# LayerNorm statistics of one token tile moved to ScalarE, and two of three warm-up matmuls taken out of a transformer block's prologue

## The chip, the cores and the metric

One core of a Trainium2 chip. The metric is the device time of one execution in microseconds (us). A time quoted here is a median of several executions; the profile is that of one execution, and its span is 1.7 to 1.9 us shorter than that execution's time (805.0 us of span went with 806.83 us). "Granted clock" is the mean share of TensorE's full speed over an execution. The experiments were made in five calls on four chips, each call with the kernel before beside them, so times are compared within a call. Every execution counts as fast; for e7 and e8, one execution each, the state is unknown.

## The reference

One block: attention with 32 heads of 16 columns over 2048 tokens of 512 columns, then a gated MLP, both behind a LayerNorm that is scaled and shifted by six vectors made from a condition `c`.

```python
def reference(A_x, A_wqkv, A_wo, B_x, B_w_gate, B_w_up, B_w_down, c, w_mod):
    x = A_x
    mod = (_silu(c) @ w_mod).reshape(c.shape[0], 6, 1, -1)
    sa, ca, ga, sb, cb, gb = ...                      # six vectors of 512
    h = _layernorm(x, axis=-1) * (1 + ca) + sa
    x = x + ga * attention(h, A_wqkv, A_wo)           # H = 32, Dh = 16, softmax over 2048 keys
    h = _layernorm(x, axis=-1) * (1 + cb) + sb
    x = x + gb * (_gelu(h @ w_gate) * (h @ w_up) @ w_down)
    return x
```

## The kernel before

The program is written as one stream of recorded operations. A small model of the engines orders them on the host ahead of time. In the main loop ScalarE takes the exponentials of all scores (686 instructions, most of 1024 or 1536 columns), while TensorE makes scores and value products. The prologue has to produce the first scores: LayerNorm of four token tiles of 128 rows, the modulation columns, transposes, the first projections.

```python
        self.warm_up(7)
        # ... cut: identity and masks on GpSimd
        for dc in range(NDC):
            self.mm(self.scp[:, 0, dc:dc + 1], self.crow[0:1, P * dc:P * dc + P], self.ones[0:1, 0:1])
        self.warm_up(14)
        self.act(self.tcol[:, :], self.scp[:, 0, 0:NDC], ACT.Tanh, scale=0.5)
        for t in range(2):
            self.ln_stat(t)                     # VectorE: statistics of tiles 0 and 1
        self.ln_rstd(0, 2)                      # GpSimd: 1 / standard deviation
        # ... cut: silu of c
        for t in range(2, 4):
            self.ln_stat(t)                     # VectorE: tiles 2 and 3
        self.ln_rstd(2, 4)
        self.mod_cols(self.scp[:, 1, 0:8], 0)   # TensorE: 32 products, wait for w_mod
        for t in range(4):
            self.ln_norm(t, self.tb1[:, 0, t, :])
        self.copy(dve, self.modA[:, :], self.scp[:, 1, 0:8])
        self.ts(dve, self.modA[:, 4:8], self.modA[:, 4:8], 1.0, None, ALU.add)
        self.warm_up(3)
        # ... cut: 16 transposes, each group of 4 followed by its modulation; then the projections

    def warm_up(self, n):
        for _ in range(n):
            self.mm(self.mi[:, :], self.warm[:, 0:P], self.warm)   # becomes 4 quarter products of 512 columns

    def ln_stat(self, t, src=None):
        s6 = self.st6[:, t % 2, :]
        self.bn_stats(s6, self.xs[:, t, :] if src is None else src)
        self.bn_aggr(self.mv[:, t, :], s6)
```

One part of the host's model of TensorE matters later. It counts every matmul (`fetched[0]`, from 0) and lets every 128th start no sooner than 3750 ns after the 128th before it:

```python
            if self.fetched[0] % 128 == 0 and t > 20000:
                t = self.fetched[1] = max(t, self.fetched[1] + 3750)
            self.fetched[0] += 1
```

So a change of the number of matmuls in the prologue changes what this model expects, and with it the order that it chooses, some 750 us later.

## Time and profile before

| | before |
|---|---|
| time, median of 3 (lowest to highest) | 807.34 us (806.82 to 807.36) |
| span of the profiled run | 805.0 us |
| first exponential starts | 13.51 us |
| ScalarE busy, TensorE busy | 96%, 93% of the span |
| modulation columns start (TensorE), "M" below | 7.66 us |

The profile is read as follows. The chain that ended last says what the end waited for. A timeline row is start, length, engine, source line, operation, the tile written and the tile read, shapes, count, and in brackets how long the engine stood idle ahead of it and what released it; `<-issue` means that no semaphore wait explains the idle time. Names of tiles: `xs` tokens, `st` and `mv` statistics, `dreg` the normalized tokens (and the warm-ups' operand), `sc_bf,mreg` the modulation columns, `hreg,wreg` the first projections, `ps_pv<-E,vaug` value products, `ps_sc<-xs,ident` fillers of the main loop. A warm-up group of 4 quarter products takes 0.43 us while the array runs at half clock and 0.22 us at full clock. The lines themselves stand in the prediction.

### The profile page before, as it was taken

To read this page: it belongs to the slowest core of one execution; us is meant where nothing else is said; L and a number is where in the kernel's file an instruction comes from. 1 tells how busy PE (TensorE), PEld (TensorE's weight loads), DVE (VectorE), ACT (ScalarE), POOL (GpSimd) and SP (SyncE) were. 2 spreads that over 40 slices of the span, in tenths; PEclk is the share of its full clock that TensorE was granted. 3 is DMA by queue.
4 is the path that set the end of the run, shared out by engine and by line. 5 is a ranking of instruction groups with operands and counts; after the bars stand their busy time and mean duration, and the time that the engine had idled before them with its cause. 6 is when DMAs were issued, how large, how long until landed. Compare 5 with 4: busy or idle time off the path is not lost.

```text
span 805.0 us, 27412 instructions
## 1 busy us (share of the span) xinstructions
PE 749.6 (93%) x12250; PEld 267.6 (33%) x12254; DVE 671.0 (83%) x1216; ACT 773.7 (96%) x728; POOL 277.7 (34%) x172
## 2 busy tenths in 40 slices
PE   8899999998899999999999899999999899999987
PEld 3333333322222222222222222222344342454455
DVE  7878898978898989988688998989778986677873
ACT  5999999999999999999999999999999999999982
POOL 3110335365546172456556346134262010000310
PEclk9999999999999999999999999999999999999999
DMA  9101000000022121111003111110123221120100
GB/s 310 58 9 19 10 10 16 10 16 10 16 55 68 35 55 36 48 41 29 24 27 108 36 52 51 48 42 17 42 59 89 63 75 37 34 75 14 23 9 14
DMA packets 58632, 36.03 MB, mean 45 GB/s; under 512 B 17977, under 2 KB 55090, under 8 KB 58514
## 3 DMA queue, kind: packets, MB, share of 16 engines
q1 hardware_dynamic: 56914, 32.84, 15.0%
q8 instruction: 96, 1.57, 0.8%
q10 hardware_dynamic: 1600, 1.44, 0.6%
q14 instruction: 22, 0.18, 0.1%
HBM read 29.62 MB, written 2.61 MB: 40 GB/s over the span
## 4 chain that ended last, share of the span: by engine, by line
ACT 89%; PE 8%; DVE 3%; issue 0%; DVEq 0%
ACT E L381 85%; PE ps_sc L368 4%; ACT wreg L381 3%; PE ps_mi L368 3%; PE ps_pv L368 1%; DVE mreg L393 1%; DVE kmo L402 0%; DVE xs L385 0%; DVE wreg L385 0%; PE ps_sc L372 0%; DVE hreg L393 0%; ACT L381 0%; DVE vaug L402 0%; DVE dreg L393 0%; DVE kme L393 0%
## 5 line engine op out<-in xcount | busy, mean ns | idle before, releaser
L381 ACT ACTIVATE E<-ps_sc 128x1024 bf16<-128x1024 f32 (+2 forms) x686 | 748.2, 1282 | 15.6 <-PE ps_sc L368 15.0
L393 POOL TENSOR_SCALAR mreg<-dreg 128x2048 uint16<-128x2048 uint16 x93 | 175.3, 1902 | 260.7 <-DVE mreg L393 105.7
L393 DVE TENSOR_SCALAR dreg<-ps_sc 128x512 uint16<-128x512 f32 x253 | 171.6, 685 | 34.3 <-PE ps_sc L368 31.8
L368 PE MATMUL ps_sc<-qT,kme 32*128 32x512 bf16 (+2 forms) x1313 | 168.3, 332 | 18.3 <-ACT E L381 15.1
L368 PE MATMUL ps_sc<-qT,kmo 32*128 32x512 bf16 (+2 forms) x1313 | 173.7, 332 | 9.7 <-ACT E L381 8.5
L368 PE MATMUL ps_pv<-E,vaug 128*17 128x512 bf16 (+2 forms) x2112 | 150.4, 327 | 0.8 <-DVE osb L402 0.5
L393 POOL TENSOR_SCALAR mreg<-mreg 128x2048 uint16<-128x2048 uint16 x46 | 86.7, 1902 | 138.8 <-DVE mreg L393 47.1
L368 PE MATMUL ps_pv<-mreg,vaug 128*17 128x512 bf16 (+2 forms) x1704 | 121.6, 337 | 1.7 <-DVE mreg L393 1.0
L393 DVE TENSOR_SCALAR mreg<-ps_sc 128x512 uint16<-128x512 f32 x126 | 85.4, 686 | 18.9 <-PE ps_sc L368 17.5
L368 PE MATMUL ps_mi<-wreg,mreg 128*32 128x512 bf16 (+1 forms) x1280 | 92.4, 372 | 4.4 <-DVE wreg L398 1.3
L368 PEld LDWEIGHTS ps_sc<-qT,kme 32*128 32x128 bf16 x1313 | 45.0, 91 | 143.7 <-ACT E L381 115.4
L368 PEld LDWEIGHTS ps_sc<-qT,kmo 32*128 32x128 bf16 x1313 | 45.7, 91 | 127.8 <-ACT E L381 109.3
L393 DVE TENSOR_SCALAR mreg<-dreg 128x2048 uint16<-128x2048 uint16 x117 | 76.8, 682 | 1.7 <-PE ps_pv L368 1.4
L368 PEld LDWEIGHTS ps_pv<-E,vaug 128*17 128x17 bf16 x2112 | 43.9, 89 | 61.5 <-issue 48.8
L368 PEld LDWEIGHTS ps_pv<-mreg,vaug 128*17 128x17 bf16 x1704 | 38.1, 89 | 36.8 <-issue 13.2
L402 DVE CAST wreg<-ps_mi 128x512 bf16<-128x512 f32 x49 | 33.5, 684 | 10.5 <-PE ps_mi L368 10.3
L368 PEld LDWEIGHTS ps_mi<-wreg,mreg 128*32 128x32 bf16 x1280 | 26.7, 95 | 44.0 <-issue 18.8
L368 PE MATMUL ps_mi<-hreg,wreg 128*32 128x512 bf16 x480 | 39.5, 385 | 0.0
L393 DVE TENSOR_SCALAR mreg<-mreg 128x2048 uint16<-128x2048 uint16 x59 | 38.4, 682 | 1.1 <-PE ps_pv L368 1.0
L398 DVE SCALAR_TENSOR_TENSOR wreg<-wreg,ps_mi 128x512 bf16<-128x512 bf16 x49 | 33.4, 682 | 6.5 <-PE ps_mi L368 5.1
L635 POOL TENSOR_SCALAR mv<-mv 128x4 f32<-128x4 f32 (+2 forms) x11 | 2.6, 239 | 94.5 <-DVE mv L425 93.9
L385 DVE TENSOR_TENSOR wreg<-wreg 128x1024 bf16<-128x1024 bf16 (+1 forms) x56 | 34.1, 616 | 0.5
(149 smaller groups left out, 670.8 us busy)
## 6 DMA issues: line engine op xcount, KB each, us to landing
mreg<-in_B_w_up_dram SPq DMA_DIRECT2D x22, 256.0 KB, 2.9
mreg<-in_B_w_gate_dram SPq DMA_DIRECT2D x15, 256.0 KB, 3.0
rb<-scr_rec SPq DMA_DIRECT2D x96, 32.0 KB, 1.8
dreg<-in_B_w_down_dram SPq DMA_DIRECT2D x9, 256.0 KB, 3.0
mreg<-in_w_mod_dram SPq DMA_DIRECT2D x1, 2048.0 KB, 13.3
mreg<-in_B_w_down_dram SPq DMA_DIRECT2D x8, 256.0 KB, 2.7
out_dram<-xs SPq DMA_DIRECT2D x16, 128.0 KB, 1.7
osb<-osb SPq DMA_DIRECT2D x48, 32.0 KB, 2.0
```

Of the source, the lines that this page charges most:

```text
L368: return self.rec("pe", lambda e: e.matmul(out, lhsT, rhs, start=start, stop=stop, tile_position=tp), [lhsT, rhs], [out], cost=(n, int(rhs ...
L381: return self.rec("act", lambda e: e.activation(out, in_, func, scale=scale, **kw), rd, wr, cost=self.cost("act", out, [in_], "act"))
L385: return self.rec(eng, lambda e: e.tensor_tensor(out, a, b, op), [a, b], [out], cost=self.cost(eng, out, [a, b], "tt"))
L393: return self.rec(eng, lambda e: e.tensor_scalar(out, a, s1, s2, **kw), rd, [out], cost=self.cost(eng, out, [a], "ts"))
L398: return self.rec("dve", lambda e: e.scalar_tensor_tensor(out, a, s, b, op0=op0, op1=op1), rd, [out], cost=self.cost("dve", out, [a, b], " ...
L402: return self.rec(eng, lambda e: e.tensor_copy(out, in_), [in_], [out], cost=self.cost(eng, out, [in_], "ts"))
L635: self.rec("pool", lambda e: e.tensor_scalar(v, v, EPS, None, op0=ALU.add), [v], [v], cost=200)
```

## The change

The intent: the statistics of tile 3 are the last on VectorE; ScalarE is idle then and can make a sum and a sum of squares with its accumulating output, so that VectorE has three tiny instructions left. The warm-ups ahead of the transposes then would be the only thing in the way, so two of three go. Both parts aim at an earlier first exponential.

```diff
         self.act(self.tcol[:, :], self.scp[:, 0, 0:NDC], ACT.Tanh, scale=0.5)
+        self.act(self.E[:, 0, :], self.xs[:, 3, :], ACT.Copy, accum=self.rden[:, 0, 0:1])
+        self.act(self.E[:, 0, :], self.xs[:, 3, :], ACT.Square, accum=self.rden[:, 0, 1:2])
 ...
-        for t in range(2, 4):
-            self.ln_stat(t)
+        self.ln_stat(2)
+        m, q, v = self.rden[:, 0, 0:1], self.rden[:, 0, 1:2], self.mv[:, 3, 1:2]
+        self.ts(dve, self.mv[:, 3, 0:1], m, 1.0 / D, None, ALU.mult)
+        self.stt(v, m, 1.0 / D, self.mv[:, 3, 0:1], ALU.mult, ALU.mult)
+        self.stt(v, q, 1.0 / D, v, ALU.mult, ALU.subtract)
         self.ln_rstd(2, 4)
 ...
-        self.warm_up(3)
+        self.warm_up(1)
```

The order of instructions also changes near the end (767 us), because the host's model counts 8 matmuls fewer.

In the prediction, the marked cuts are statements that no trace or run of this case shows. No term of its sum rests on them: it stays 0.37 + 0.24 = 0.61 us, 806.73 us in all, and the 0.70 us taken for each of ScalarE's two instructions is from the trace (695 ns).

> **What bounds the kernel now.** I read the page first (busy shares, then the chain that ended last), then that chain in order of time for the first 32 us and for the last 50, then the timelines of VectorE, GpSimd, TensorE and ScalarE in those two stretches.
>
> The page, busy line of ScalarE and the chain by engine:
>
> ```profile
> span 805.0 us, 27412 instructions
> ...
> ACT 89%; PE 8%; DVE 3%; issue 0%; DVEq 0%
> ```
>
> ScalarE's exponentials set the time: 89% of the chain. They can't start before the prologue has produced the first scores, so the prologue's length (first exponential at 13.51 us) is added to the whole, and whatever shortens it should come off the end one for one. Between 13 and 70 us the view of waits lists no wait for a DMA, so no arrival is there to swallow an earlier start. The chain in the prologue:
>
> ```profile
> 4.59 3.13 PE ps_mi L368 x56
> 7.73 0.89 PE ps_sc L368 x32
> 8.62 0.76 PE ps_mi L368 x12
> 9.38 1.00 PE ps_sc L372 x16
> 10.38 0.39 PE ps_pv L368 x4
> ```
>
> TensorE alone is named: 14 warm-ups, the 32 columns of the modulation, three more warm-ups (12 quarter matmuls), 16 transposes, projections. But the timeline of VectorE and GpSimd shows a second path that ends almost together with it:
>
> ```profile
> 6.43 0.18 DVE L425 BATCH_NORM_AGGREGATE mv<-st 128x2 f32<-128x6 f32 x1
> 6.53 0.66 DVE L421 BATCH_NORM_STATS2 st<-xs 128x6 f32<-128x512 bf16 x1
> 7.22 0.18 DVE L425 BATCH_NORM_AGGREGATE mv<-st 128x2 f32<-128x6 f32 x1
> 7.49 0.30 POOL L635 TENSOR_SCALAR mv<-mv 128x2 f32<-128x2 f32 x1 [0.85 <-DVE mv L425]
> 7.88 0.73 POOL L637 TENSOR_TENSOR rstd<-mv,half 128x2 f32<-128x2 f32 x1
> 8.64 0.74 DVE L393 TENSOR_SCALAR dreg<-xs,mv,rstd 128x512 bf16<-128x512 bf16 x2 [0.61 <-POOL rstd L637]
> 9.29 0.16 DVE L402 COPY modA<-ps_sc 128x8 f32<-128x8 f32 x1
> 9.48 0.17 DVE L393 TENSOR_SCALAR modA<-modA 128x4 f32<-128x4 f32 x1
> 9.76 1.00 DVE L393 TENSOR_SCALAR hreg<-ps_sc,modA 128x512 bf16<-128x512 bf16 x2
> ```
>
> Statistics of tile 3 end at 7.40, rstd of tiles 2 and 3 at 8.61, their norms at 9.05 and 9.38, modA at 9.65. And TensorE in two narrow windows, around 9.0 and 9.48:
>
> ```profile
> 8.99 0.39 PE L368 MATMUL ps_mi<-dreg 128*32 128x512 bf16 x4
> ...
> 9.31 0.40 PE L372 MATMUL ps_sc<-ident,dreg 128*128 128x128 bf16 x4
> ```
>
> The third warm-up starts at 8.99 and takes 0.2 us of issue; the transposes start at 9.31, some 0.06 apart, the fourth at 9.49, when tile 3's norm (9.38) had been ready for 0.1 us. So the warm-ups set the transposes, with the statistics path 0.05 us behind; the fourth's end (9.71) releases the modulate at 9.76. Neither part of the change can give much alone.
>
> One more place, near the end: the chain there, and one filler of the main loop.
>
> ```profile
> 754.72 12.23 ACT E L381 x11
> 766.94 0.04 issue
> 766.98 0.78 PE ps_sc L368 x11
> ...
> 767.99 9.99 ACT E L381 x8
> ```
> ```profile
> 766.98 0.62 PE L368 MATMUL ps_sc<-xs,ident 128*32 128x512 bf16 x8 [0.52 <-ACT E L381]
> 767.53 0.23 PE L368 MATMUL ps_sc<-qT,kme 32*128 32x128 bf16 x3
> ```
>
> Two filler products (8 quarter matmuls) stand between the release of a score buffer and the scores that ScalarE needs next. Exponentials of 1024 columns follow each other at 0.90 us (765.78, 766.68); the next could have started at 767.59, and started at 767.98.
>
> [...] The trace has 598 ns from PSUM and 695 ns for a 128x512 tile in SBUF; I take 0.70. [...] Built, the changed kernel has the same two table loads as before, so none is added (1.28 us each in this trace). [...] in the trace a dependent small instruction starts 0.19 us after the one before (9.29 to 9.48). [...] the trace agrees on the two speeds (first 7 warm-ups 3.1 us, 0.43 each; the next 14 take 3.13, 0.22 each).
>
> **The change part by part.** (a) Off VectorE: tile 3's statistics, 0.66 + 0.18 us, at 6.53 to 7.40.
>
> (b) On ScalarE: Copy and Square of tile 3 with sums. ScalarE is idle from 4.80 to 9.97. The tile's DMA was issued at 1.21 and landed 3.5 us later, at 4.71. So the Copy runs 4.80 to 5.50, the Square, which waits for it, about 5.55 to 6.25; with an unknown cost for each sum, by 6.6. VectorE needs the first sum at 6.53 and the second at 6.91: hidden.
>
> (c) On VectorE instead: three dependent 128x1 instructions, at 6.53, 6.72, 6.91, ending near 7.07. GpSimd gets its input at 7.07 instead of 7.40: -0.33 us. Then as before: 0.09 + 0.30 + 0.09 + 0.73, rstd at 8.28; norms at 8.31 and 8.64, ending 8.72 and 9.05; modA copy at 8.96, plus one at 9.15, ending 9.32.
>
> (d) TensorE: one warm-up at 8.54 (0.22) plus the 0.11 seen before the transposes gives the first at 8.87; the fourth waits for tile 3's norm: 9.05 + 0.06 = 9.11, ending 9.33. The modulate starts at 9.38, when modA is ready too. That is 9.76 - 9.38 = 0.38 us earlier. The warm-ups cut alone would leave the fourth transpose at 9.38 + 0.06 = 9.44 (-0.05); the statistics alone would leave it at 9.49 (0).
>
> (e) After it nothing new: the K weights landed at 2.17 + 7.3 = 9.47, before the first projection's new time of 9.98. First exponential at about 13.14. I count 0.37 us.
>
> (f) The order of instructions, from the built kernels: identical on every engine after the prologue up to about 767 us. There the static scheduler leaves out the two fillers at 766.98, and VectorE does one score conversion ahead of a small product and another small product earlier. Without the fillers the scores start at 766.98; their third bank waits for a conversion that ends at 767.00, so they are complete near 767.45 and ScalarE can start at 767.59: up to 0.39 us. But TensorE then is busy without a gap to the scores at 770.15, and the filler there (768.09) still waits for the exponential that ends at 767.85. It moves only to 767.90, so those scores come 0.19 us earlier, complete near 770.42, and the exponential that was at 770.66 starts there: 0.24 us of the 0.39 stay. From 767.98 to 777.98 ScalarE has no gap, and the tail follows it.
>
> Sum: 0.37 + 0.24 = 0.61. 807.34 - 0.61 = 806.73 us.
>
> **The rivals.** First, the prologue's gain is lost because the warm-ups were needed: with fewer columns between 7.7 and 10.0 us the clock could halve for one window, in which the projections (1.76 us) would take twice as long. For it: little else runs on the array there. Against it: the stretch that starts at 11 us is no busier and kept 0.22 us per group. The time would be 807.5 to 809, perhaps in some runs only. Second, ScalarE's sums come late (a hidden cost of reading them out, or a later landing of tile 3), and VectorE waits: each 0.1 us past 6.9 costs 0.1; at 0.3 late the prologue gives nothing, and the time is 807.1. Third, the gap at 767 closes less because a VectorE conversion comes later in the new order: prologue alone, 806.97. Fourth, all 0.39 stays: 806.58.
>
> **Range and chances.** The three runs before spread over 0.54 us, near the size of the gain, so the median carries some 0.2 of noise. With the rivals, 806.2 to 807.3 should hold it 8 times in 10; most of the rest lies above. Two per cent is 16 us; no mechanism here reaches it. I give faster 0.005, within 2% 0.985, slower 0.01 for something unforeseen.
>
> **What would show it.** In the profile after: Square ending before 6.9; the last small statistics instruction ending near 7.07; rstd at 8.3; modulate at 9.4; first exponential near 13.1; the exponential at 767.98 now near 767.2 (both shifts together) and the last one 0.6 earlier. Projections at 0.43 us per group would prove the clock rival. A wait of VectorE for ScalarE ahead of the small instructions would prove the second. A first exponential at 13.1 with an unchanged end would mean that a fixed arrival took the gain back, and the statement on DMA waits would be wrong.

## The result, and the profile after

| | before, same call | after |
|---|---|---|
| time, median of 4 | 807.35 us (806.82 to 807.46) | 807.39 us (806.53 to 808.79) |
| ratio of fast runs, 95% interval | | 1.0003, 0.9986 to 1.0021 |
| span of the profiled run | 805.0 us | 806.9 us |
| M, first exponential, distance | 7.66, 13.51, 5.84 us | 8.21, 13.62, 5.41 us |
| from the first exponential to the end | 791.45 us | 793.33 us |

A ratio here is the mean time of one kernel's fast runs over that of the other's in the same rounds, so it isn't quite the ratio of the medians beside it. The change isn't seen in the time at all; 806.73 us was predicted, and the measured median lies 0.09 us above the upper end of the range of 806.2 to 807.3.

The page of the kernel after (the span, the queue of kind "instruction", the shares of the chain that ended last):

```profile
span 806.9 us, 27386 instructions
...
q8 instruction: 96, 1.57, 0.8%
...
ACT 86%; PE 9%; DVE 3%; DMA 1%; SPq 1%; issue 0%; DVEq 0%
```

ScalarE still carries the chain, but DMA and the sequencer of SyncE are new in it with 1% each. The chain in order of time, kernel after, prologue (start, length, what):

```profile
4.61 3.67 PE ps_mi L368 x56
8.27 0.88 PE ps_sc L368 x32
9.16 0.33 PE ps_mi L368 x4
9.49 1.00 PE ps_sc L372 x16
10.49 0.37 PE ps_pv L368 x4
```

The third row has 0.33 us where the kernel before had 0.76: the two warm-ups are gone, and what follows M is shorter by 0.43 us. But the first row is longer by 0.54 us (3.67 after 3.13). Same work, 14 groups, but ten of the first 21 groups ran wholly or partly at half clock in this execution and seven in the other (the granted clock doubled at 5.66 us here and at 4.29 us there). That lies ahead of the changed part, and in this one execution it took the gain back before that part had begun.

ScalarE's timeline in the kernel after, with the two sums:

```profile
4.79 0.63 ACT L381 ACTIVATE E<-xs 128x512 bf16<-128x512 bf16 x1
5.33 0.19 ACT L381 ACTIVATION_READ_ACCUMULATOR E<-xs 128x1 f32 x1
5.54 0.63 ACT L381 ACTIVATE E<-xs 128x512 bf16<-128x512 bf16 x1
6.08 0.19 ACT L381 ACTIVATION_READ_ACCUMULATOR E<-xs 128x1 f32 x1
```

Each sum is read out by an instruction of its own, 0.19 us; all is over at 6.27. And VectorE in the kernel after, the three tiny instructions, the norms and the modulation vector:

```profile
6.32 0.12 DVE L393 TENSOR_SCALAR mv<-rden 128x1 f32<-128x1 f32 x1
6.47 0.35 DVE L398 SCALAR_TENSOR_TENSOR mv<-rden,mv 128x1 f32<-128x1 f32 x2
...
8.09 0.73 DVE L393 TENSOR_SCALAR dreg<-xs,mv,rstd 128x512 bf16<-128x512 bf16 x2 [0.61 <-POOL rstd L642]
9.20 0.17 DVE L402 COPY modA<-ps_sc 128x8 f32<-128x8 f32 x1 [0.38 <-PE ps_sc L368]
```

No wait for ScalarE stands ahead of them, the statistics end at 6.82 and the last norm at 8.82. VectorE then waits 0.38 us for TensorE's modulation columns: in this execution the statistics path isn't near the critical path any more.

To see where the later time went, the k-th exponential of one trace was set beside the k-th of the other (both have 686), and the lag of the kernel after was followed. These are the steps over 0.2 us, and the first and the last lag:

```
exponential   start before   start after   lag
0                13.51         13.62       0.11
221, 222        248.82, 249.73 249.56, 251.08   0.12 -> 1.35
667 to 669      763.45 - 765.78  764.88 - 767.70  1.23 -> 1.92
671             767.98        769.52       1.94 -> 1.55
676             774.65        776.56       1.67 -> 1.91
end             804.96        806.95       1.99
```

At 248 us the array runs a window at half clock (granted clock 0.5 for 3.41 us), in the middle of the unchanged main loop: eight fillers take 1.03 us, 0.61 in the kernel before. At 671 is the predicted gain of two missing fillers, -0.39 us. The step at 676 goes with a round trip of the softmax denominators through memory, one leg of which took 3.3 us in this trace; its cause was not tested (e4 below has a step of 0.28 us there too, behind a stall of 0.60 us at the 11842nd matmul). At 667 to 669 is something else. TensorE's timeline in the kernel after:

```profile
762.13 0.34 PE L368 MATMUL ps_pv<-E,vaug 128*17 128x128 bf16 x10
763.13 0.28 PE L368 MATMUL ps_pv<-E,vaug 128*17 128x128 bf16 x6 [0.66 <-issue]
...
766.29 0.35 PE L368 MATMUL ps_pv<-E,vaug 128*17 128x128 bf16 x12
766.87 0.23 PE L368 MATMUL ps_pv<-E,vaug 128*17 128x128 bf16 x4 [0.23 <-issue]
```

and the first of these two runs of 16 value products in the kernel before:

```profile
760.97 0.60 PE L368 MATMUL ps_pv<-E,vaug 128*17 128x128 bf16 x16
```

After the change the same run of products is broken in two, with 0.66 us of idle time in its middle and no semaphore that it waits for. The stall comes at matmul number 11458 of the trace, counted from 0, the next one at number 11586: 128 apart. In the kernel before, the run took 0.60 us where its neighbours take 0.40: number 11458 lies in it too, near its start, and came 0.20 us after the matmul before it. These stalls are what the experiments had to explain.

### The profile page after: what moved, and what is told of

Same layout as the page of the kernel before. It is cut to its first block, busy times and chain, and to the rows that moved or that the text cites. A ratio compares the mean times of both kernels' runs of the same rounds, so it can differ in the third digit from the quotient of the medians.

```text
span 806.9 us, 27386 instructions
## 1 busy us (share of the span) xinstructions
PE 750.0 (93%) x12234; PEld 267.4 (33%) x12238; DVE 671.3 (83%) x1217; ACT 775.8 (96%) x732; POOL 277.4 (34%) x172
## 3 DMA queue, kind: packets, MB, share of 16 engines
q8 instruction: 96, 1.57, 0.8%
## 4 chain that ended last, share of the span: by engine, by line
ACT 86%; PE 9%; DVE 3%; DMA 1%; SPq 1%; issue 0%; DVEq 0%
ACT E L381 83%; PE ps_sc L368 4%; PE ps_mi L368 3%; ACT wreg L381 3%; PE ps_pv L368 1%; DVE mreg L393 1%; SPq L432 1%; DMA scr_rec<-rden 0%; DMA den<-scr_den 0%; DMA rb<-scr_rec 0%; DVE kmo L402 0%; DVE xs L385 0%; DVE dreg L393 0%; PE ps_mi L372 0%; DVE wreg L385 0%
```

## The experiments

Eighteen runs were made; all were correct. "Stretch" is the time from the first exponential to the end in the profiled run, "M" the start of the modulation columns. Comparing M, M to first exponential, and stretch keeps apart what the times mix. Each of these three comes from one execution of each kernel.

### 1. Are these two traces typical? The same kernels again, and each half of the program alone

e1 is the kernel before without an edit, e2 the kernel after. e3 and e4 use the fact that the host's model only counts matmuls: shifting its count by 8 gives the end order of one kernel to the other.

```diff
# e3: prologue before, end order after        # e4: prologue after, end order before
         self.prologue()                               self.prologue()
+        self.fetched[0] -= 8                 +        self.fetched[0] += 8
         self.stream()                                 self.stream()
```

> The kernel before, unchanged, as a control. All theories: ratio 1.000 to the kernel before, within what the rounds scatter. Its trace gives a second look at when the array's clock doubles in the warm-ups: if the doubling comes at another moment than 4.5 us, the first exponential moves from 13.51 us by 0.21 us per slow group of four warm-up matmuls (theory A, a clock phase that differs from run to run); if it stays at 13.51 whatever the phase, theory A falls.

> The changed kernel, unchanged. Theory A (both steps of the prediction are real and each about as large as predicted; the single profiled run hid them behind a late doubling of the clock, 0.55 us, one slow clock window at 248 us, 1.24 us, and late denominators near the end, 0.8 us): ratio about 0.9993 (-0.6 us), 0.9989 to 0.9997. Theory B (the filler's gain is swallowed by the wait for the denominators' round trip; the prologue's is real): -0.37 us, 0.9995. Theory C (8 matmuls fewer ahead of everything shift where TensorE's stream of instructions stalls, and stalls at 762 and 766 us now lie on the path in every run): ratio about 1.000, with TensorE waits of 0.6 us marked as issue at the same two places.

> The kernel before with only the order near the end as in the changed kernel (two fillers fewer, one conversion and one product moved), prologue untouched. Theory A: -0.24 us, ratio 0.9997, and in the trace the exponential after the missing fillers 0.39 us closer to the one before it, of which the exponential two places on gives back 0.15. Theory B: the same step in the trace, but ScalarE waits that much longer for the scores behind the denominators at about 774 us: ratio 1.000. Theory C: 1.000, no stall at 762.

> Both parts of the change in the prologue, with the order near the end kept as before. Theories A and B: -0.37 us, ratio 0.9995; first exponential near 13.1 us if the clock doubles by 4.5 us, up to 13.6 if it doubles at 5.7. Theory C: stalls of TensorE marked as issue at 762 and 766 us as in the changed kernel's trace, ratio about 1.0002.

| run | M | M to first exponential | stretch | median (5 runs) | ratio to before |
|---|---|---|---|---|---|
| e1 | 8.84 | 5.90 | 791.52 | 807.21 | 0.9992 (0.9980 to 1.0005) |
| e2 | 9.07 | 7.33 | 791.24 | 807.08 | 0.9996 (0.9983 to 1.0009) |
| e3 | 7.66 | 5.98 | 791.22 | 807.11 | 0.9993 (0.9980 to 1.0006) |
| e4 | 8.31 | 5.41 | 791.74 | 807.21 | 0.9990 (0.9977 to 1.0004) |

The unedited kernel before has the ratio 0.9992: times of this kind can't tell effects of half a microsecond apart. The traces can. e1 shows that M is no property of the kernel: it lay at 7.66 in one execution and at 8.84 in another, with thirteen groups wholly or partly at half clock in place of seven. e3 gives the end's gain by itself: stretch 791.22 after 791.45, -0.23 us, against 0.24 predicted. e4 gives the prologue's by itself: 0.43 us are gained from M to the first exponential, and the stretch is 0.29 us longer, with stalls at numbers 11458 and 11842. e2 shows that the kernel after doesn't lose in every execution: no such stall of 0.33 us or more between 740 and 785 us, and a stretch of 791.24 us, that of e3.

M to the first exponential is longer than 5.84 or 5.41 us where the second half of the weights lands after M, so that TensorE waits among the columns. Measured from the start of the last of the 32 columns, the distance is 5.05 to 5.06 us in all seven traces without either part or with the statistics alone (before, e1, e3, e5, e7, e13, e16), 4.84 us with the warm-ups alone (e8), and 4.62 to 4.63 us in all nine with both parts (after, e4, e6, e9 to e12, e17, e18); the traces in which the array fell to half clock in the prologue (e2, e14, e15) are left out.

In e2 the modulation weights landed late, at 8.93 and 9.42 us. TensorE in that trace:

```profile
9.07 0.19 PE L368 MATMUL ps_sc<-sc_bf,mreg 128*128 128x1 bf16 x2 [1.32 <-DMA mreg<-in_w_mod_dram]
...
12.23 0.64 PE L368 MATMUL ps_sc<-hreg,wreg 128*32 128x512 bf16 x4
...
14.78 0.38 PE L368 MATMUL ps_sc<-hreg,wreg 128*32 128x512 bf16 x4
```

After 1.32 us of waiting the array falls back to half clock, from 11.34 to 14.76 us (0.64 us for a group of projections in place of 0.38 at the end) and the first exponential comes 1.57 us late (6.19 us after the last column in place of 4.62). That is the first rival of the prediction, in one execution of the kernel after.

### 2. Fixing the start: a gate

To take the scatter of the clock's doubling and of the weights' landing out, a gate holds VectorE back until long after both: more warm-ups, one product into another bank, and a VectorE copy of that bank ahead of the statistics. It costs some 7 us and is the same in each.

```diff
# e5: before with a gate (the count is set so that the end order stays that of before)
+        self.fetched[0] -= 132
-        self.warm_up(7)
+        self.warm_up(34)
+        self.mm(self.scp[:, 4, :], self.warm[:, 0:P], self.warm)
+        self.warm_up(5)
         ...
+        self.copy(dve, self.st6[:, 0, 0:4], self.scp[:, 4, 0:4])
         for t in range(2):
             self.ln_stat(t)
# e6: the same gate, both parts of the change;  e7: statistics part alone, warm_up(3);  e8: warm-up part alone
```

> The kernel before with 33 groups of warm-up matmuls more at the start, and the first statistics held until six groups before the conditioning matmuls, so that the array's clock has doubled and all early transfers have landed when the measured stretch begins; order near the end kept. Theory A (the start of the modulation columns moves with the clock's doubling and with w_mod's landing, and that is most of the scatter): the modulation columns start straight after the 14 warm-ups, and from their start to the first exponential it takes 5.85 us as in the first trace; the five times scatter less than the 2.2 us of the ungated kernel, under 1 us unless a slow clock window falls in. Rival (the scatter comes from elsewhere, the middle or the end): the same scatter as before.

> The same gate with both parts of the change. Theory A: from the start of the modulation columns to the first exponential 5.47 us (0.38 less than the gated kernel before) if the statistics path still binds, 5.41 if the warm-up does; end of the program earlier by as much in the trace outside slow clock windows. Rival: the gain at the first exponential is there but is gone at the last one.

> The gate with ScalarE's statistics alone and three warm-ups. Prediction's step (d): no gain, 5.85 us from the modulation columns to the first exponential, because the transposes stay behind the third warm-up. Rival: the statistics are the path and give 0.3 us alone.

> The gate with one warm-up and the statistics on VectorE as before. Prediction's step (d): 0.05 us, 5.80, because the fourth transpose waits for tile 3's norm. Rival, suggested by the ungated traces in which the modulation columns started late: the warm-ups alone give the whole 0.43 us.

| run | M | M to first exponential | stretch | median |
|---|---|---|---|---|
| e5 before | 16.16 | 5.84 | 791.48 | 814.48 |
| e6 both | 16.20 | 5.41 | 791.92 | 814.10 |
| e7 statistics alone | 14.75 | 5.84 | 791.46 | 813.88 (one run) |
| e8 warm-ups alone | 15.97 | 5.62 | 792.04 | 815.47 (one run) |

The prologue does what was predicted: both parts together 0.43 us, statistics alone nothing, warm-ups alone half (0.22; there the fourth transpose starts 0.06 us after the last norm, so the statistics path holds it). But the stretch is longer by 0.44 us in e6 and by 0.56 us in e8, and unchanged in e7. So the loss, called the give-back below, goes with the cut of the warm-ups, that is with eight matmuls fewer in TensorE's stream. (M itself differs by up to 1.45 us among the four: the doubling of the clock falls at other times, between 4.22 and 7.15 us, so the medians mean little. The five times of e5 still spread over 1.18 us, where under 1 us was expected.)

### 3. Putting the eight matmuls back where they cost nothing

Two warm-up groups are put behind the first projections, where TensorE is idle (0.80 us in the kernel after), without the host's model being told.

```diff
# e9: e6 with the padding;  e10: e9 with the end order of the kernel after;
# e11: e4 with it;  e12: the kernel after with it
         # after the first projections
+        kept = (dict(self.free), self.pe_issue, self.pe_end, ...)   # the model's state
+        self.warm_up(2)
+        self.free, self.pe_issue, self.pe_end, ... = kept
```

> The gate with both parts of the change, and the 8 warm-up matmuls that the change takes away put back where TensorE stands idle, after the projections. Theory C' (taking 8 matmuls away moves all later code against fixed places in TensorE's stream, 128 matmuls apart, where it stalls; in five of five traces with the cut the stalls at two such places near the end sum to 0.5 to 1.4 us, in five of five without it to 0.05 to 0.3): the stalls at those places return to under 0.3 us and the end of the trace is earlier than the gated kernel before by the prologue's 0.43 us, about 814.0 in the clean runs. Rival (the late stalls are chance, or come from the earlier start itself): they stay near 1.1 us and the end is level with the gated kernel before.

> As the run before, with the changed kernel's order near the end (two fillers fewer) as well. Theory C': another 0.24 us, 0.6 to 0.7 in all against the gated kernel before. Rival: stalls of 0.5 us or more near the end, no gain.

> No gate: the changed prologue with the 8 matmuls put back after the projections, order near the end as before. Theory C': 0.43 us under the kernel before in the mean, ratio 0.9995, scatter of 0.5 us a run as in all ungated kernels; in the trace 5.41 us from the modulation columns to the first exponential and stalls under 0.3 us at the fixed places near the end. Rival: ratio 1.000 with stalls of 1 us.

> The candidate for a better kernel: as the run before, with two fillers fewer near the end. Theory C': 0.67 us under the kernel before, ratio 0.9992; the exponential after the missing fillers 0.39 us closer to its forerunner. Rival: 1.000.

| run | M to first exponential | stretch | median | ratio to before |
|---|---|---|---|---|
| e9 | 5.41 | 791.46 | 814.08 | 1.0082 |
| e10 | 5.41 | 791.31 | 814.55 | 1.0087 |
| e11 | 5.65 | 791.44 | 806.53 | 0.9991 (0.9978 to 1.0003) |
| e12 | 5.85 | 791.60 | 806.19 | 0.9988 (0.9976 to 1.0001) |

With the end order of before, the stretch is back to 791.46 and 791.44: the loss is gone and the prologue's gain stays (5.65 in e11, where the weights landed late, at 8.38). With the end order of after the padding isn't clean. In e10 -0.17 us stay against e5, though its median is 0.47 us above that of e9, and in e12 a stall of 0.45 us at the 11586th matmul eats the end's gain in the profiled run. e12 has the best median of all kernels, 806.19 us (four of its five runs between 806.14 and 806.43), against 807.36 us of the kernel before in the same call; its interval ends at 1.0001, so a gain of 1 us is likely and not proven, the less so as it is the best of several kernels that were tried.

### 4. Eight matmuls fewer, and nothing else

e13 is e5 with 32 warm-ups in place of 34 ahead of the gate, where no part of the change is; the order on every engine is that of e5.

```diff
-        self.fetched[0] -= 132
+        self.fetched[0] -= 124
-        self.warm_up(34)
+        self.warm_up(32)
```

> The prologue of the kernel before with the same gate as e5, but with 8 quarter matmuls (2 warm-up groups) taken out of the warm-ups ahead of the gate, where no part of the change sits. Nothing else differs from e5: same order on every engine. Theory (stalls at fixed places 128 matmuls apart): the distance from the start of the modulation columns to the first exponential stays at 5.84 us; the stalls near 760 to 775 us have the sizes seen with 8 matmuls cut (one of 0.5 to 0.9 us), and the stretch from the first exponential to the end is 0.3 to 0.6 us longer than in e5. Rival (the shortened prologue itself, by the time at which ScalarE starts relative to VectorE or to transfers, makes the loss): this run has the prologue of e5 in all its distances, so the stretch from the first exponential to the end is that of e5 within 0.1 us.

M to the first exponential is 5.85 us as in e5, and the stretch 791.99: 0.51 us longer, with a prologue that is otherwise unchanged (median 814.74 us, ratio 1.0087, as e5's). TensorE in e5, two runs of value products:

```profile
769.53 0.40 PE L368 MATMUL ps_pv<-E,vaug 128*17 128x128 bf16 x16
...
773.29 0.40 PE L368 MATMUL ps_pv<-E,vaug 128*17 128x128 bf16 x16
```

and the same two in e13:

```profile
768.44 0.28 PE L368 MATMUL ps_pv<-E,vaug 128*17 128x128 bf16 x6
769.03 0.34 PE L368 MATMUL ps_pv<-E,vaug 128*17 128x128 bf16 x10 [0.30 <-issue]
...
772.25 0.29 PE L368 MATMUL ps_pv<-E,vaug 128*17 128x128 bf16 x8
773.05 0.29 PE L368 MATMUL ps_pv<-E,vaug 128*17 128x128 bf16 x8 [0.51 <-issue]
```

The rival, that a shorter prologue as such shifts ScalarE against transfers, is out: no step of the prologue was shortened here, and e9 and e11 have the shortened prologue without the loss. Nor is it the earlier start, 1.02 us ahead of e5's: e7 started 1.41 us ahead and lost nothing.

### 5. What sits at every 128th matmul

The page lists 96 packets and 1.57 MB of kind "instruction" on one queue, so 16 KB each; 12234 matmuls in the kernel after make 95.6 groups of 128. With the 12238 weight loads of the same page that is some 255 TensorE instructions to a packet, an estimate from these counts. Between 740 and 785 us, all traces together (before, after, e1 to e18) have 19 gaps of 0.33 us or more between two matmuls that no semaphore explains. A gap is taken from start to start. All 19 are at a place with the number 66 plus a multiple of 128, and each place starts 1.21 to 1.59 us after such a packet has landed. Every trace has as many packets on this queue as such places (96, and 97 in the gated kernels), and, but for the last two places, exactly one lands between each place and the next. From the trace of the kernel after:

```
packet of 16 KB         next place            gap to the matmul before it
760.25 to 761.60        11458 at 763.13       0.88
764.26 to 765.63        11586 at 766.87       0.45
```

The second packet starts 1.13 us after the first place was passed, takes 1.37 us, and the next place follows 1.25 us later: 3.75 us in all. In the four cases in which two places in a row stalled, they lie 3.75 to 4.02 us apart. Ahead of that stretch 128 matmuls take longer than that (5.1 to 7.1 us at 740 to 760 us), and no place there has a gap over 0.23 us in the traces of the kernels before and after; from 760 to 780 us the scores are of 128 columns, and 128 matmuls took 2.9 us where no place stalled (11714 to 11842 in the kernel before). The author's reading is that a packet brings the instructions of 128 matmuls and that TensorE here gets to the next 128 before their packet is in. The traces show the order and the distances; that the packet which lands is the one that the stalled matmul waits for was not shown. Where a place falls in that stretch would then decide whether the stall lies in slack or on the path to the next exponential. Eight matmuls fewer move it by half a run of 16 value products.

It isn't a matter of place alone. A packet took between 0.88 and 1.96 us, and the stalls scatter: e2, with eight fewer, had none over 0.33 us, and e14 (below), with none cut, had two. Over the traces with the end order of before, the stretch is 791.44 to 791.52 us in six with the full number of matmuls (before, e1, e5, e7, and the padded e9 and e11) and 791.86 in e14; in the five with eight fewer it is 791.74 to 792.23 (e4, e6, e8, e13, e15). With the end order of after, the loss came in one of two executions of the kernel after: none in e2, and in the first profile some 0.9 us against e3 (793.33 less 1.23 for the half-clock window is 792.10, against 791.22).

### 6. Does the cut of the warm-ups make the half clock more frequent?

Here the two transfers of the modulation weights are issued behind those of the projection weights, so that they land late in every execution. e14 has the prologue before, e15 the one after, both with the end order of before.

```diff
-        self.dma(act, self.wmod[0][:, 0:2, :], wmv[:, 0:2, 0:1024], "wm0")
-        self.dma(sp, self.wmod[0][:, 2:4, :], wmv[:, 2:4, 0:1024], "wm2")
         for k, q in ((1, sp), (0, act), (2, sp)):
             self.dma(q, wq4[:, :, k, 0:P], wqv[:, :, k, 0:P], "wq%d" % k)
         self.dma(act, self.xs[:, 4:8, :], xv[:, 4:8, :], "x2")
+        self.dma(act, self.wmod[0][:, 0:2, :], wmv[:, 0:2, 0:1024], "wm0")
+        self.dma(sp, self.wmod[0][:, 2:4, :], wmv[:, 2:4, 0:1024], "wm2")
```

> The kernel before with the two transfers of the modulation weights issued last of the prologue's, so that they land late in every run. Serves as the base of e15. The modulation columns should start near 9 us, after TensorE has waited for the weights for 1 us or more; distance from there to the first exponential 5.84 to 5.9 us; clock at least 0.999 in most executions if three warm-up groups keep it up.

> e14 with the change's prologue and the end order of before. Theory A (the warm-ups were not needed): distance from the start of the modulation columns to the first exponential 5.41 us, and most executions at a clock of 0.999 or more, median within 0.4 us of e14. Theory B (with weights late, one warm-up group is too little and the clock halves for a window, as in the profile of e2): projections at 0.43 us per group, distance 6.9 to 7.3 us, clock 0.997 or 0.998 in more executions than in e14, median 0.7 to 1.5 us above e14.

e14 took 811.74 us (809.67 to 813.25), e15 811.96 us (810.88 to 813.05); M to the first exponential was 8.05 and 7.56 us in the profiles, with M at 11.10 and 10.54 us where some 9 was expected. Both expectations missed in part: the half clock came in both. TensorE in e14:

```profile
11.10 0.19 PE L368 MATMUL ps_sc<-sc_bf,mreg 128*128 128x1 bf16 x2 [2.63 <-DMA mreg<-in_w_mod_dram]
...
12.69 1.34 PE L368 MATMUL ps_mi<-dreg 128*32 128x512 bf16 x12
```

Three warm-up groups stand there and take 0.43 us each: behind the wait of 2.63 us for the weights the clock is already halved when they begin, so they don't prevent it. The granted clock was 0.998 or less in 4 of 6 executions of e14 and in 5 of 5 of e15; that doesn't tell them apart. Whether one group in place of three makes the halving more frequent at shorter waits stays open. What the two show is that behind late weights it came with either number; of the 11 executions of the kernel before in the same call none was at 0.998 or less.

### 7. A plan with the true places

The host's model already has places every 128 matmuls, but it counts from 0 and the traces have them at 66 plus a multiple of 128. Started at 62, the count agrees with the traces, and only the order near the end changes. e16 is the kernel before with it, e17 the kernel after, e18 e12.

```diff
-        self.fetched = [0, 0.0]
+        self.fetched = [62, 0.0]
```

> The kernel before, whose static scheduler already keeps a minimum of 3.75 us between every 128th matmul, but counts from 0, while in every trace the stalled places are those with the number 66 plus a multiple of 128. Here the scheduler's count starts at 62, so that its places fall on those of the traces; only the order of the last 50 us changes. Theory [...]: [...] the scheduler now plans with them; first exponential to end at most 791.4 us, 0.1 to 0.5 less than the 791.45 to 791.52 of the kernel before. Rival (the order itself counts more than where the blocks end): stretch of 791.5 to 792.5 with new waits of ScalarE between 760 and 782 us.

> The kernel after with the same shift of the scheduler's count, so that the eight missing matmuls are planned with at their true places. Theory: no give-back, first exponential to end at most 791.4 us and within 0.2 of e16; distance from the modulation columns to the first exponential 5.41 us; over all 0.3 to 0.5 us under e16 when the columns start at the same time. Rival: give-back as before, stretch of 791.7 us or more, no gain over e16.

> e12 (both parts, eight matmuls put back in idle time after the projections, which the scheduler does not count) with the scheduler's count started at 62. Its plan is that of e17, but the true places fall 8 matmuls earlier in it than planned. Theory: where the plan is 8 matmuls off, stalls of 0.3 to 0.9 us may return on the path: stretch 0 to 0.6 us longer than e17. Rival (phase does not matter): stretch as e17 within 0.1 us.

| run | M to first exponential | stretch | median (4 runs) | ratio to before |
|---|---|---|---|---|
| e16 | 5.84 | 792.69 | 808.04 | 0.9997 (0.9979 to 1.0015) |
| e17 | 6.00 | 791.58 | 807.04 | 0.9984 (0.9966 to 1.0001) |
| e18 | 5.53 | 792.51 | 807.45 | 0.9989 (0.9969 to 1.0009) |

The theory's expectation failed. The stalls are indeed small (none over 0.33 us in e16 and e18, one of 0.33 in e17), but the stretch isn't shorter. In e18 the profiled run has a half-clock window near 533 us that accounts for 1.11 us of the lag, so 791.40 without it. In e16 the new order has a new wait:

```profile
773.59 0.40 PE L368 MATMUL ps_mi<-wo,onorm 128*32 128x512 bf16 x4 [0.74 <-DVE onorm L385]
...
774.36 0.62 PE L368 MATMUL ps_sc<-qT,kmo 32*128 32x128 bf16 x24
```

TensorE waits 0.74 us for a normalized output ahead of the scores that ScalarE needs; 0.91 us of lag come at that one exponential. The rival of e16 is right: what else the order does weighs more than the phase, that is, where in the order the places fall. The orders of e16 and e17 differ from each other from 762 us on, so their stretches can't be set against each other; e17 and e18 have the same order. e18 was to bring the stalls back at a phase that is off by eight, and didn't. So in the order of before the number of matmuls ahead decides whether the give-back comes (e6, e8, e13 with eight fewer; e9 and e11 with the eight put back), as far as one trace of each can show it; e14 is the exception, and there is no general rule for planning with it.

## Why the prediction was wrong, and where it was right

**Steps (a) to (c), the statistics: right, with spare time.** ScalarE's sums end at 6.27 (6.25 to 6.6 was said), the statistics at 6.82 (7.07), rstd at 8.05 (8.28); some 0.2 us of these are an earlier start of VectorE's work in this execution. The second rival, late sums, did not come.

**Step (d), 0.38 us: right in size.** Both parts give 0.43 from M to the first exponential in the trace after, e4, e6, e9 and e10. Statistics alone give 0 as said. "The warm-ups cut alone" was put at 0.05 and is 0.22 in e8: the norm of tile 3 ends 1.72 us after M in the trace before and 1.50 after M in e8, and this distance isn't fixed: the norm follows the token tile's landing (or the gate), M the warm-ups and the weights.

**The unspoken part of step (d): wrong.** It took M as 7.66 us, from one trace. M lay between 7.66 and 9.07 in ungated executions of the original transfer order, with seven to thirteen groups wholly or partly at half clock and weights landing between 7.45 and 9.42 us. In the trace after, M came 0.55 us later, more than the 0.43 gained; that was bad luck and not the change, since the kernel before has it too (8.84 in e1).

**Step (e), "After it nothing new": the step that failed.** It followed the wait list to 70 us and the order of instructions, found both clean, and kept 0.37 us to the end; with the end's 0.24 us that made 0.61, where the medians show none (0.04 us more). Eight matmuls fewer move every later place of section 5 within the order; between 760 and 780 us stalls of 0.4 to 0.9 us then hold up the scores that ScalarE waits for (in e13 one exponential falls back by 0.65 us against e5). The stretch grows by 0.29 (e4), 0.44 (e6), 0.51 (e13) and 0.56 us (e8): most of the prologue's gain, or more than it. With the eight put back it grows by nothing (e9, e11). The prediction's sign for this, an earlier first exponential with an unchanged end, did come (e6 against e5: 0.39 us earlier at the first, 0.05 later at the end), but it laid that to the arrival of a fixed transfer. The kernel's own code has a term for such places: the model's 3750 ns for every 128th matmul. The prediction noticed that the order changes and didn't ask why the count of matmuls should change an order at all.

**Step (f), 0.24 us: right in size when nothing stalls.** -0.39 us at the exponential behind the missing fillers, +0.18 two further on, -0.23 in the stretch of e3. The third and fourth rivals did not come.

**The first rival, half a window of clock: real, with too little weight.** It came in the profiled run of e2 (1.6 us in the prologue, with 3.42 us at half clock) and, in the profiled run after, in the main loop at 248 us (1.2 us), where the prediction didn't look. Nothing says that it is the change's doing there: of 54 executions of the kernel before in all calls, six took 808.37 us or more, each at a granted clock of 0.998 or less, and the other 48 took 808.15 or less. Two of the nine of the kernel after are of this kind (808.79 and 809.37).

**The range: too narrow.** "0.2 of noise" was read from three runs that spread over 0.54 us. Executions without such a window alone spread from 806.60 to 808.15 us in the kernel before. The predicted gain of 0.61 was the sum of two right terms; a third term of 0.29 to 0.56 us of loss (measured in the end order of before; 0 and some 0.9 in the two traces of the kernel after) was missing, so some 0.05 to 0.3 us may be left, and that is under the scatter of a median of four. The seven undisturbed executions of the kernel after have a mean of 807.05 us and the 48 of the kernel before one of 807.45, which fits a small gain; they are from several calls, and no interval of one call shows it.

## What to carry to other kernels

When a change is worth less than the scatter of the times, compare traces instruction by instruction, from one milestone to the next, and run the unchanged kernel as well: M alone moved here by more than the gain. Taking matmuls out of TensorE's stream also moved where in the order the stalls at every 128th matmul fall; if a later stretch does 128 matmuls in less time than stalled places lie apart (2.9 us against 3.75 to 4.02 here), try to pad the removed ones back into idle time, and look at that stretch again. And if a static scheduler changes its order without an apparent reason, find out which term of its model moved.
